# Routing one-hots moved from GpSimd to VectorE, routing steps and a gather moved earlier, in a one-core attention and mixture-of-experts kernel

## The chip, the core and the metric

The kernel runs on one core of a Trainium2 chip. The metric is the device time of one execution in microseconds (us), the median of several executions. Inputs are drawn once and kept.

## What is computed

The reference is block-causal attention over 8 sequences of 576 tokens with 8 heads of width 64, followed by a mixture of 8 experts. A token's expert is its id times a constant, modulo 8, which is the low three bits of the id; no gate is learned, so the routing does not depend on the attention.

```python
scores = scale * np.matmul(q, k.transpose(0, 1, 3, 2))      # 8 x 8 x 576 x 576
scores = np.where(block_i >= block_j, scores, -1000000000.0) # blocks of 64
attn = softmax(scores)
x = (attn @ v) as 4608 x 512
expert_idx = token_ids * np.int64(2654435761) % np.int64(8)
for e in range(8):
    xe = x[expert_idx == e]
    out[expert_idx == e] = np.maximum(xe @ w1[e], 0.0) @ w2[e]   # 512 -> 1024 -> 512
```

## The kernel before, in words

**Attention** is done in 32 pairs of heads, four pairs to a sequence. The loop at L583 runs over steps g = 0 to 33, and g // 4 is the sequence. A step computes the scores of pair g in three chunks (`S_chunk`, L212 and L221, exponential on ScalarE at L238), multiplies the exponentials of pair g - 2 with the values (`PV`, L276 and L279), divides by the row sums (`norm`, L286 and L287) and then makes small pieces of other work in the order in which they are written: transposes of the next sequence's q and k (`T_group`, L180 on TensorE, L187 on VectorE; eight "eighths" per sequence, dealt to the last two or three steps of the sequence before by the table `turned`), the cast of the values on GpSimd (`cast_v`, L155 and L158), loads of sequence b + 2 (`load_seq`, where g is a multiple of 4) and the write of a finished sequence to a DRAM buffer `x_dram` (`write_x`, L301). `fill` (L205) issues products of zeros into a scratch bank; nothing reads them.

**Routing** is a Python generator, `route` (L318). Every `next(rgen)` emits the instructions up to the next `yield`. It extracts the expert of every token, counts tokens per expert with two small matmuls (L353, L354), gives every token a slot (`slot_i`, 640 slots per expert and an overflow area), and then inverts this: for each of the 8 sequences it builds one-hot matrices of the slot's low 7 bits (128 wide) and high part (72 wide, times the two digits of the token's number), and a TensorE product of the two (L465) adds the token numbers into a table in slot order, `tabi`. The one-hots are built on GpSimd by four element-wise instructions each (`equal`, L442 to L447) and a product (L455). Each sequence takes three `next` calls; the loop makes four calls in steps 0 and 1 and one in each later step.

**Experts.** `load_x` gathers the token rows of expert e from `x_dram` into the tile `xg` by indirect DMAs of 128 rows (L310), five per expert. The first three (the early slots, GE = 3) hold only rows of sequences 0 to 5, so they may be gathered before the last two sequences are written; the last two (late) may not. `turn_x` transposes xg (L503, copy at L505), `stage_a` (L655; `stage_a_early` at L510) multiplies by w1 with a ReLU, `stage_b` (L671) by w2, copies the result (L678) and scatters it to the output (L680). During step 29 expert 0's early rows are turned, during steps 30 to 32 its first product is made. After the loop come the late gathers of experts 0 and 1, and then the experts in turn: while expert e is multiplied, w1, w2 and xg of expert e + 2 are requested, in that order. The turns of expert e + 1 stand between the products of expert e's `stage_b`.

**Queues.** Each engine runs its instructions in the order written. GpSimd (POOL) issues the loads of q, k, w1, w2 and all indirect DMAs from the same stream as its arithmetic; SyncE (SP) issues the loads of v and the writes of `x_dram`. A load of k waits until the values of the sequence before it have landed (`after`). Buffers: two of q, k, v, three of each weight and of xg, two score banks, two banks for transposes and one-hot products (`psT`), one output bank pair (`psO`).

## Time and profile before

| | us |
|---|---|
| median of 3 executions | 352.18 (350.62 to 352.39) |
| the profiled execution, its own time | 354.03 |
| its span, first to last instruction | 352.4 |
| TensorE busy (matmul) | 281.5 |
| GpSimd busy | 210.1 |
| VectorE busy | 148.5 |
| ScalarE busy | 144.0 |

The profile gives the busy time of the engines (PE is TensorE, PEld its weight loads, DVE VectorE, ACT ScalarE, POOL GpSimd), the TensorE clock that was granted (PEclk: 1.00 is 2.4 GHz, 0.50 is 1.2 GHz, a mean in between is a mix of the two), and for each idle stretch of an engine which other engine's work ended it. Busy time of a matmul group is modelled, so it is read beside waits, not alone.

### The profile page before, as it was taken

To read this page: it belongs to the slowest core of one execution; us is meant where nothing else is said; L and a number is where in the kernel's file an instruction comes from. 1 tells how busy PE (TensorE), PEld (TensorE's weight loads), DVE (VectorE), ACT (ScalarE), POOL (GpSimd) and SP (SyncE) were. 2 spreads that over 40 slices of the span, in tenths; PEclk is the share of its full clock that TensorE was granted. 3 is DMA by queue.
4 is the path that set the end of the run, shared out by engine and by line. 5 is a ranking of instruction groups with operands and counts; after the bars stand their busy time and mean duration, and the time that the engine had idled before them with its cause. 6 is when DMAs were issued, how large, how long until landed. Compare 5 with 4: busy or idle time off the path is not lost. (4 is left out here: it accounts for less than half of the span.)

```text
span 352.4 us, 7677 instructions
## 1 busy us (share of the span) xinstructions
PE 281.5 (80%) x3218; PEld 181.8 (52%) x3234; DVE 148.5 (42%) x298; ACT 144.0 (41%) x181; POOL 210.1 (60%) x235
## 2 busy tenths in 40 slices
PE   4858888857756865983989891999999999999980
PEld 1526666635535634762665550465656556565630
DVE  3698596647246326762462121313222231405130
ACT  1573868845534723883424330041323314050600
POOL 7224399999999999615202862757475748414140
PEclk9886999998678868797699996799999999999997
DMA  7999998639619716997702799989999999912020
GB/s 111 189 217 187 195 235 162 136 63 199 115 26 202 136 44 159 190 200 173 162 3 84 124 247 237 183 268 178 256 161 274 181 269 174 266 47 114 15 106 30
DMA packets 65111, 55.63 MB, mean 158 GB/s; under 512 B 39973, under 2 KB 53797, under 8 KB 65072
## 3 DMA queue, kind: packets, MB, share of 16 engines
q0 software_dynamic: 22560, 40.90, 55.5%
q1 hardware_dynamic: 42512, 14.20, 18.3%
...
## 5 line engine op out<-in xcount | busy, mean ns | idle before, releaser
L238 ACT ACTIVATE pt<-ps 128x1024 bf16<-128x1024 f32 x96 | 93.4, 1023 | 67.0 <-PE ps L221 65.8
L659 ACT ACTIVATE hT<-hp 128x640 bf16<-128x640 f32 (+2 forms) x70 | 42.9, 613 | 105.7 <-PE hp L655 104.8
L671 PE MATMUL yp<-w2b,hT 128*128 128x512 bf16 x305 | 76.2, 389 | 0.8
L680 POOL DMA_INDIRECT out_dram<-ysb,perm x40 | 39.9, 998 | 52.9 <-DVE ysb L678 24.9
L655 PE MATMUL hp<-xT,w1b 128*128 128x320 bf16 (+2 forms) x472 | 66.7, 296 | 3.8 <-DVE xT L505 3.6
L310 POOL DMA_INDIRECT xg<-x_dram,tabi x40 | 41.0, 1025 | 43.4 <-DMA x_dram<-xs 31.3
L505 DVE COPY xT<-tx 128x512 bf16<-128x512 bf16 x40 | 16.9, 425 | 101.1 <-PE tx L503 101.1
L187 DVE COPY qkT<-tp 128x640 bf16<-128x640 bf16 (+1 forms) x60 | 50.3, 876 | 18.4 <-PE tp L180 18.1
L655 PEld LDWEIGHTS <-w1b 128*128 128x128 bf16 x472 | 45.6, 98 | 22.6 <-issue 5.7
L671 PEld LDWEIGHTS <-hT 128*128 128x128 bf16 x320 | 30.8, 100 | 31.9 <-issue 2.8
L212 PE MATMUL ps<-qkT 64*128 64x512 bf16 (+4 forms) x320 | 43.6, 336 | 3.0 <-ACT pt L238 1.2
L276 PE MATMUL O<-vx,pt 128*128 128x65 bf16 x896 | 44.2, 206 | 2.2 <-DVE xs L287 1.9
L276 PEld LDWEIGHTS <-pt 128*128 128x128 bf16 x896 | 36.2, 105 | 9.3 <-DVE xs L287 3.9
L678 DVE COPY ysb<-yp 128x512 f32<-128x512 f32 x40 | 27.3, 682 | 12.2 <-PE yp L671 12.2
L212 PEld LDWEIGHTS <-qkT 64*128 64x128 bf16 x320 | 19.2, 103 | 18.6 <-issue 6.5
L287 DVE TENSOR_TENSOR xs<-O,rsall 128x640 bf16<-128x640 f32 x32 | 26.4, 824 | 1.1
L221 PE MATMUL ps<-maskq,maskk 64*128 64x64 bf16 x256 | 26.4, 209 | 0.4 <-issue 0.4
L503 PE MATMUL tx<-identbf,xg 128*128 128x128 bf16 x160 | 16.4, 230 | 12.4 <-DMA xg<-x_dram,tabi 12.3
L503 PEld LDWEIGHTS <-xg 128*128 128x128 bf16 x160 | 12.5, 102 | 21.6 <-DMA xg<-x_dram,tabi 13.4
L180 PE MATMUL tp<-identbf,kb 128*64 128x128 bf16 x288 | 16.1, 255 | 4.5 <-DVE qkT L187 3.2
...
L286 DVE RECIPROCAL rsall<-O 128x10 f32<-128x10 f32 x32 | 6.7, 211 | 27.1 <-PE O L279 26.8
...
## 6 DMA issues: line engine op xcount, KB each, us to landing
...
w1b<-in_moe_w_dram POOLq DMA_DIRECT2D x8, 1024.0 KB, 8.3
w2b<-in_moe_w_dram POOLq DMA_DIRECT2D x8, 1024.0 KB, 13.1
...
vf<-in_v_dram SPq DMA_DIRECT2D x16, 64.0 KB, 4.0
xg<-x_dram,tabi POOLq DMA_INDIRECT x40, 10.0
```

The source lines that it names most:

```text
L187: ins = copy(qk[:, :, w, :].rearrange("p h (g j) -> p h g j", j=JR)[:, :, :, j0 + c0 : j0 + c1], tp[:, at[c0] : at[c1 - 1] + 1, :].rearran ...
L212: nc.tensor.matmul(ps[:, m, o0 : o0 + n], lhsT=qk[rows, r, 1, 128 * i : 128 * i + 128], rhs=qk[rows, r, 0, q0 : q0 + n], start=True, stop= ...
L221: nc.tensor.matmul(ps[:, m, o0 : o0 + 64], lhsT=maskk[rows, :], rhs=maskq[rows, :], start=False, stop=True,)
L238: nc.scalar.activation(ptv[:, :, 512 * ch : 512 * ch + 512], ps[:], ACT.Exp, scale=SCALE)
L276: nc.tensor.matmul(dst, lhsT=pt[:, o0 : o0 + 128], rhs=vx[:, h, i, :], start=(i == 0), stop=(i == t))
L310: r = nc.gpsimd.indirect_dma_start(out=xgs[e][:, gg, :], out_offset=None, in_=x_dram[0:rows, :], in_offset=bass.IndirectOffsetOnAxis(ap=ta ...
L503: nc.tensor.transpose(out=tp[:, db, :], in_=xgs[e][:, tt, db * P : (db + 1) * P], identity=identbf[:])
L655: nc.tensor.matmul(hp[:, t, 0:n], lhsT=w1b[:, db, ft * P : (ft + 1) * P], rhs=xT[:, db, p0:p1], start=(db == 0), stop=(db == NKT - 1),)
L659: nc.scalar.activation(hT[:, ft, c0:c1].rearrange("p (t n) -> p t n", n=n), hp[:, 0 : len(parts), 0:n], ACT.Relu)
L671: nc.tensor.matmul(yp[:], lhsT=hT[:, ft, tt * P : (tt + 1) * P], rhs=w2b[:, ft, :], start=(ft == 0), stop=(ft == NFT - 1),)
L678: nc.vector.tensor_copy(ysb[:], yp[:])
L680: ins = nc.gpsimd.indirect_dma_start(out=out[:, :], out_offset=bass.IndirectOffsetOnAxis(ap=perm3[:, gg : gg + 1], axis=0), in_=ysb[:], in ...
```

## The change

The one-hots are built by VectorE, with `is_equal` against a bf16 counting tile `iota_c` in which every number stands five times, so that the five tokens of a partition are the innermost dimension; three VectorE instructions per sequence take the place of nine on GpSimd. They come before the small tables of `route` and take one `next` per sequence. Before the first transposes the generator is now called four times, with 28 zero products among the calls (11 before); the calls left over are dealt to steps by the table STEPS. The arithmetic on `toki` moves behind the first transposes. Sequence 2's transposes are dealt to three steps as those of the later ones are. The early rows of expert 2 are gathered in step 28, its late rows beside those of experts 0 and 1 after the loop. Expert 0's turn moves from step 29 to 28, its first product from steps 30 to 32 to steps 29 to 31.

```diff
@@ -398,6 +398,41 @@
         nc.vector.tensor_copy(slot_i[:].rearrange("p b i -> p (b i)"), slf[:])
         yield
 
+        lo_i = rt.tile([P, 2, T], I32, name="lo_i", tag="i2")
+        nc.vector.tensor_single_scalar(lo_i[:, 0, :], slot_i[:].rearrange("p b i -> p (b i)"), 127, op=ALU.bitwise_and)
+        nc.vector.tensor_single_scalar(lo_i[:, 1, :], slot_i[:].rearrange("p b i -> p (b i)"), 7, op=ALU.arith_shift_right)
+        dig = rt.tile([P, 2, B, 5], BF16, name="dig")
+        nc.vector.tensor_copy(dig[:].rearrange("p z b i -> p z (b i)"), lo_i[:])
...
+        ones_hi = rt.tile([P, NG, 5], BF16, name="ones_hi", tag="oh")
+        hots = rt.tile([P, 2, P + 2 * NG, 5], BF16, name="hots", tag="tid")
+        yield
+        for b in range(B + 1):
+            if b > 0:
+                hot = hots[:, (b - 1) % 2]
+                pt_ = psT.tile([P, 512], F32, name="pt_", tag="tp")
+                for i in range(5):
+                    n = P if i < NT else 64
+                    nc.tensor.matmul(pt_[:, 0 : 2 * NG], lhsT=hot[0:n, 0:P, i],
+                                     rhs=hot[0:n, P:, i], start=(i == 0), stop=(i == 4))
+                if b == 1:
+                    nc.vector.tensor_copy(acc[:], pt_[:, 0 : 2 * NG])
+                else:
+                    nc.vector.tensor_tensor(out=acc[:], in0=pt_[:, 0 : 2 * NG], in1=acc[:], op=ALU.add)
+            if b < B:
+                nc.vector.tensor_tensor(
+                    out=hots[:, b % 2, 0:P, :], in0=dig[:, 0, b, None, :].to_broadcast([P, P, 5]),
+                    in1=iota_c[:], op=ALU.is_equal)
+                nc.vector.tensor_tensor(
+                    out=ones_hi[:], in0=dig[:, 1, b, None, :].to_broadcast([P, NG, 5]),
+                    in1=iota_c[:, 0:NG, :], op=ALU.is_equal)
+                nc.vector.tensor_tensor(
+                    out=hots[:, b % 2, P:, :].rearrange("p (z h) i -> p z h i", z=2),
+                    in0=ones_hi[:, None, :, :].to_broadcast([P, 2, NG, 5]),
+                    in1=tokb[:, b, :, None, :].to_broadcast([P, 2, NG, 5]), op=ALU.mult)
+                yield
+        yield
+
         eo = rt.tile([1, OVT, E], F32, name="eo")
         nc.vector.tensor_tensor(
             out=eo[:], in0=inc[0:1, None, :].to_broadcast([1, OVT, E]),
@@ -425,49 +460,6 @@
         yield
...
-        dif = rt.tile([P, 5, P], BF16, name="dif", tag="oh")
-        hots = rt.tile([P, 2, 5, P + 2 * NG], BF16, name="hots", tag="tid")
-        yield
-
-        def equal(out, z, b, n):
-
-            d = dif[:, :, 0:n]
-            nc.gpsimd.tensor_tensor(
-                out=d, in0=lo_f[:, z, b, :, None].to_broadcast([P, 5, n]),
-                in1=iota_lo[:, None, 0:n].to_broadcast([P, 5, n]), op=ALU.subtract)
-            nc.gpsimd.tensor_tensor(out=d, in0=d, in1=d, op=ALU.mult)
-            nc.gpsimd.tensor_scalar(d, d, -1.0, 1.0, op0=ALU.mult, op1=ALU.add)
-            nc.gpsimd.tensor_single_scalar(out, d, 0.0, op=ALU.max)
-
-        for b in range(B + 1):
-            if b < B:
-                equal(hots[:, b % 2, :, 0:P], 0, b, P)
-            yield
-            if b < B:
-                equal(dif[:, :, 0:NG], 1, b, NG)
-                nc.gpsimd.tensor_tensor(
-                    out=hots[:, b % 2, :, P:].rearrange("p i (z h) -> p i z h", z=2),
-                    in0=dif[:, :, None, 0:NG].to_broadcast([P, 5, 2, NG]),
-                    in1=tokf[:, b, :, :, None].to_broadcast([P, 5, 2, NG]), op=ALU.mult)
-            yield
-            if b > 0:
-                hot = hots[:, (b - 1) % 2]
...
@@ -530,17 +522,12 @@
                    allow_small_or_imprecise_dtypes=True)
-    iota_lo = rt.tile([P, P], F32, name="iota_lo")
-    nc.gpsimd.iota(iota_lo[:], pattern=[[1, P]], base=0, channel_multiplier=0,
+    iota_c = rt.tile([P, P, 5], BF16, name="iota_c")
+    nc.gpsimd.iota(iota_c[:], pattern=[[1, P], [0, 5]], base=0, channel_multiplier=0,
                    allow_small_or_imprecise_dtypes=True)
     toki = rt.tile([P, B, 5], I32, name="toki")
     nc.gpsimd.iota(toki[:], pattern=[[S, B], [P, 5]], base=0, channel_multiplier=1,
                    allow_small_or_imprecise_dtypes=True)
-    tok2 = rt.tile([P, B, 5, 2], I32, name="tok2")
-    nc.vector.tensor_single_scalar(tok2[:, :, :, 0], toki[:], 6, op=ALU.arith_shift_right)
-    nc.vector.tensor_single_scalar(tok2[:, :, :, 1], toki[:], 63, op=ALU.bitwise_and)
-    tokf = rt.tile([P, B, 5, 2], F32, name="tokf")
-    nc.vector.tensor_copy(tokf[:], tok2[:])
     set_fixed()
 
     vparts = {0: load_v(0, firsts[2])}
@@ -560,26 +547,37 @@
     for m in range(2):
         nc.vector.memset(maskk[64 * m : 64 * m + 1, 64:128], NEG)
         nc.vector.memset(maskq[64 * m : 64 * m + 1, :], 1.0)
-    fill(9)
+
+    fill(8)
     rgen = route()
     next(rgen)
-    fill(2)
+    fill(10)
+    next(rgen)
+    fill(10)
+    next(rgen)
+    next(rgen)
     J2 = JR // 2
     T_group(0, 0, J2, 5, psS)
-    fill(1)
     T_group(0, JR, JR + J2, 5, psS)
     fill(1)
     T_group(0, J2, JR, 5, psS)
     fill(1)
     T_group(0, JR + J2, 2 * JR, 5, psS)
     cast_v(0)
+    tok2 = rt.tile([P, B, 2, 5], I32, name="tok2", tag="i2")
+    nc.vector.tensor_single_scalar(tok2[:, :, 0, :], toki[:], 6, op=ALU.arith_shift_right)
+    nc.vector.tensor_single_scalar(tok2[:, :, 1, :], toki[:], 63, op=ALU.bitwise_and)
+    tokb = rt.tile([P, B, 2, 5], BF16, name="tokb")
+    nc.vector.tensor_copy(tokb[:], tok2[:])
 
     turned = {}
     for c in range(1, B):
         f = NP * c
-        for g, ns in (((f - 2, range(0, 4)), (f - 1, range(4, 8))) if c < 3 else
+        for g, ns in (((f - 2, range(0, 4)), (f - 1, range(4, 8))) if c < 2 else
                       ((f - 3, range(0, 2)), (f - 2, range(2, 5)), (f - 1, range(5, 8)))):
             turned[g] = [(c, n) for n in ns]
+
+    STEPS = {0: 4, 1: 3, 4: 1, 8: 1, 9: 1, 12: 1, 13: 1, 16: 1, 20: 1, 21: 1, 22: 1, 23: 1, 24: 1}
     for g in range(NPAIRS + 2):
         b, r = divmod(g, NP)
         turns = list(turned.get(g, ()))
@@ -597,7 +595,7 @@
             S_chunk(g, 1)
         turn(1)
         if g < 2:
-            fill(2)
+            fill(3)
         if g >= 2:
             PV(g - 2, 0)
         if g < NPAIRS:
@@ -614,7 +612,7 @@
         if g >= 2:
             PV(g - 2, 1)
             norm(g - 2)
-        for _ in range(4 if g < 2 else 1):
+        for _ in range(STEPS.get(g, 0)):
             next(rgen, None)
         if r == 1 and g > 1:
             write_x((g - 5) // NP)
@@ -626,15 +624,16 @@
             load_w1(g // 27)
         if g == 24:
             load_w2(0)
-        if g in (NP * EB + 2, NP * EB + 3):
+        if NP * EB + 2 <= g < NP * EB + 5:
             load_x(g - NP * EB - 2, 0, GE)
 
-        if g == 29:
+        if g == 28:
             for tt in range(GE):
                 turn_x(0, tt, psT)
-        if 30 <= g < 33:
-            for ft in ((0, 1, 2), (3, 4, 5), (6, 7))[g - 30]:
+        if 29 <= g < 32:
+            for ft in ((0, 1), (2, 3, 4), (5, 6, 7))[g - 29]:
                 stage_a_early(0, ft)
+    assert next(rgen, None) is None and rgen.gi_frame is None
     att_ctx.close()
 
     ffn_ctx = ExitStack()
@@ -709,7 +708,7 @@
         nc.vector.tensor_scalar(ctl[:, 2:3], nb[:, 0:1], float(-E * G), float(E * G), op0=ALU.mult, op1=ALU.add)
         nc.vector.tensor_single_scalar(ctl[:, 3:4], nov[:], float(E * G), op=ALU.add)
 
-    for e in range(2):
+    for e in range(3):
         load_x(e, GE, G)
     load_w2(1)
     stage_a(1, 0, ES, 2)
@@ -720,7 +719,8 @@
         if e + 2 < E:
             load_w1(e + 2)
             load_w2(e + 2)
-            load_x(e + 2, 0, G)
+            if e > 0:
+                load_x(e + 2, 0, G)
         stage_a(e, ES if e < 2 else 0, CAP)
         if 1 < e + 1 < E:
             new_ffn(e + 1, mx)
```

## Rows read from the trace of the kernel before

**Rows 1.** Busy time by stage: stretch and length, PE, PEld, DVE, ACT, POOL, PEclk, DMA share, GB/s.
```profile
15.70:36.97 21.27, 15.15 (x217) 10.13 (x218) 17.65 (x46) 11.91 (x13) 7.18 (x9) 0.76 1.07 203
36.97:52.00 15.03, 12.39 (x275) 9.37 (x274) 11.81 (x28) 11.82 (x13) 10.69 (x11) 1.00 1.01 200
52.00:140.30 88.30, 61.86 (x1127) 45.31 (x1127) 44.52 (x73) 47.99 (x52) 83.01 (x83) 0.84 0.62 128
140.30:155.20 14.90, 14.50 (x275) 10.69 (x275) 12.47 (x20) 11.97 (x13) 7.75 (x10) 0.81 1.02 176
155.20:185.70 30.50, 22.91 (x324) 15.71 (x325) 12.76 (x26) 12.70 (x16) 7.06 (x7) 0.83 0.57 124
185.70:229.50 43.80, 34.73 (x207) 19.31 (x208) 9.90 (x19) 9.33 (x23) 25.62 (x26) 0.88 0.87 178
229.50:324.40 94.90, 92.47 (x613) 56.39 (x621) 25.52 (x50) 28.16 (x40) 54.32 (x56) 1.00 0.85 200
```

**Rows 2.** The same view by sequence, first and last inside the third stage.
```profile
52.00:66.15 14.15, 13.05 (x283) 9.88 (x284) 10.43 (x18) 11.76 (x13) 13.34 (x15) 1.00 0.70 162
...
115.70:140.30 24.60, 16.45 (x281) 11.97 (x277) 10.97 (x18) 12.13 (x13) 23.10 (x23) 0.78 0.59 121
```

**Rows 3.** Waits of PE from 66 to 141 us: total, times, longest.
```profile
PE pt__1765 L465 <- POOL hots L455: 4.5, 1, 4.5
...
PE pt__2140 L465 <- POOL hots L455: 3.3, 1, 3.3
```

**Rows 4.** VectorE groups, shapes kept apart: busy us, mean ns, idle before.
```profile
L187 DVE COPY qkT<-tp 128x640 bf16<-128x640 bf16 x32 | 28.9, 904 | 12.5 <-PE tp L180 12.2
...
L287 DVE TENSOR_TENSOR xs<-O,rsall 128x640 bf16<-128x640 f32 x32 | 26.4, 824 | 1.1
...
L390 DVE TENSOR_TENSOR cum<-cum,ovm 128x320 f32<-128x320 f32 x1 | 0.5, 491 | 0.0
```

**Rows 5.** Timeline of VectorE and of GpSimd near 141 us: start, duration.
```profile
140.98 2.17 DVE L471 SCALAR_TENSOR_TENSOR tabf<-acc 128x72 f32<-128x72 f32 x1
...
141.15 1.91 POOL L155 CAST vx<-vf 128x2048 bf16<-128x2048 f32 x1
```

**Rows 6.** Timeline of PE at the start.
```profile
1.36 4.02 PE L205 MATMUL fl<-wz 128*128 128x512 bf16 x9 [1.36 <-DVE wz L84]
...
9.72 1.17 PE L180 MATMUL tp<-identbf,kb 128*64 128x128 bf16 x18
...
12.95 0.69 PE L180 MATMUL tp<-identbf,kb 128*64 128x128 bf16 x18
...
15.70 0.39 PE L212 MATMUL ps<-qkT 64*128 64x512 bf16 x2 [1.11 <-DVE et L331]
```

**Rows 7.** Busy time while VectorE works at routing, L331 to L366 and L402 to L410.
```profile
15.49:20.48 4.99, 2.84 (x39) 1.78 (x40) 4.44 (x16) 3.37 (x5) 3.32 (x4) 0.92 1.08 191
...
31.27:32.46 1.19, 0.41 (x8) 0.30 (x7) 1.12 (x7) 1.19 (x2) 0.10 (x1) 1.00 1.14 214
```

**Rows 8.** Timeline of PE at expert 0's first gathered rows.
```profile
165.69 0.61 PE L503 MATMUL tx<-identbf,xg 128*128 128x128 bf16 x4 [4.10 <-DMA xg<-x_dram,tabi]
```

**Rows 9.** Timeline of PE and of POOL around expert 2's gather.
```profile
209.38 1.89 PE L671 MATMUL yp<-w2b,hT 128*128 128x512 bf16 x7
218.58 0.61 PE L503 MATMUL tx<-identbf,xg 128*128 128x128 bf16 x4 [7.31 <-DMA xg<-x_dram,tabi]
218.98 3.62 PE L671 MATMUL yp<-w2b,hT 128*128 128x512 bf16 x8
...
195.71 0.97 POOL L490 DMA_DIRECT2D w2b<-in_moe_w_dram  x1
```

**Rows 10.** DMA issues from 186 to 200 us: KB each, us to landing.
```profile
w2b<-in_moe_w_dram POOLq DMA_DIRECT2D x1, 1024.0 KB, 10.0
```

**Rows 11.** Timeline of POOL and of PE at expert 3's gathered rows.
```profile
232.94 0.98 POOL L680 DMA_INDIRECT out_dram<-ysb,perm  x1 [3.19 <-DMA xg<-x_dram,tabi]
...
240.45 0.39 PE L503 MATMUL tx<-identbf,xg 128*128 128x128 bf16 x4
```

More of the change, by code (lines that the diff above doesn't have):

```diff
@@ L399, in route @@
         yield
+        lo_i = rt.tile([P, 2, T], I32, name="lo_i", tag="i2")
[3 more added lines that the diff above has]
+        nc.vector.tensor_copy(dig[:].rearrange("p z b i -> p z (b i)"), lo_i[:])
+        acc = rt.tile([P, 2 * NG], F32, name="acc", tag="cum")
+        ones_hi = rt.tile([P, NG, 5], BF16, name="ones_hi", tag="oh")
[26 more added lines that the diff above has]
+        yield
         eo = rt.tile([1, OVT, E], F32, name="eo")
@@ L427, in route @@
         yield
-        lo_i = rt.tile([P, 2, T], I32, name="lo_i")
-        nc.vector.tensor_single_scalar(lo_i[:, 0, :], slot_i[:].rearrange("p b i -> p (b i)"), 127, op=ALU.bitwise_and)
-        nc.vector.tensor_single_scalar(lo_i[:, 1, :], slot_i[:].rearrange("p b i -> p (b i)"), 7, op=ALU.arith_shift_right)
-        lo_f = rt.tile([P, 2, B, 5], F32, name="lo_f")
-        nc.vector.tensor_copy(lo_f[:].rearrange("p z b i -> p z (b i)"), lo_i[:])
-        acc = rt.tile([P, 2 * NG], F32, name="acc", tag="cum")
-        dif = rt.tile([P, 5, P], BF16, name="dif", tag="oh")
-        hots = rt.tile([P, 2, 5, P + 2 * NG], BF16, name="hots", tag="tid")
-        yield
-        def equal(out, z, b, n):
-            d = dif[:, :, 0:n]
-            nc.gpsimd.tensor_tensor(
-                out=d, in0=lo_f[:, z, b, :, None].to_broadcast([P, 5, n]),
-                in1=iota_lo[:, None, 0:n].to_broadcast([P, 5, n]), op=ALU.subtract)
-            nc.gpsimd.tensor_tensor(out=d, in0=d, in1=d, op=ALU.mult)
-            nc.gpsimd.tensor_scalar(d, d, -1.0, 1.0, op0=ALU.mult, op1=ALU.add)
-            nc.gpsimd.tensor_single_scalar(out, d, 0.0, op=ALU.max)
-        for b in range(B + 1):
-            if b < B:
-                equal(hots[:, b % 2, :, 0:P], 0, b, P)
-            yield
-            if b < B:
-                equal(dif[:, :, 0:NG], 1, b, NG)
-                nc.gpsimd.tensor_tensor(
-                    out=hots[:, b % 2, :, P:].rearrange("p i (z h) -> p i z h", z=2),
-                    in0=dif[:, :, None, 0:NG].to_broadcast([P, 5, 2, NG]),
-                    in1=tokf[:, b, :, :, None].to_broadcast([P, 5, 2, NG]), op=ALU.mult)
-            yield
-            if b > 0:
-                hot = hots[:, (b - 1) % 2]
-                pt_ = psT.tile([P, 512], F32, name="pt_", tag="tp")
-                for i in range(5):
-                    n = P if i < NT else 64
-                    nc.tensor.matmul(pt_[:, 0 : 2 * NG], lhsT=hot[0:n, i, 0:P],
-                                     rhs=hot[0:n, i, P:], start=(i == 0), stop=(i == 4))
-                if b == 1:
-                    nc.vector.tensor_copy(acc[:], pt_[:, 0 : 2 * NG])
-                else:
-                    nc.vector.tensor_tensor(out=acc[:], in0=pt_[:, 0 : 2 * NG], in1=acc[:], op=ALU.add)
         nc.vector.scalar_tensor_tensor(out=tabf[:], in0=acc[:, 0:NG], scalar=64.0, in1=acc[:, NG:],
```

## The prediction

> **What bounds the kernel now.** The page's busy shares come first, but they are means over stages with different limits (TensorE is the busiest and GpSimd the second, as the table above shows), so I cut the span into stages [rows 1]. The reader should compare the lengths of equal work. Four steps of the attention loop (one sequence) take 15.03 us from 36.97 and 14.90 us from 140.30. The sixteen steps between take 88.30 us, 22.1 us a sequence, and there GpSimd is busy 83.01 us of the 88.30 and the granted clock is 0.84, a mix of 1.2 and 2.4 GHz. By sequence it is plainer: the first takes 14.15 us at clock 1.00, the last 24.60 us with GpSimd busy for 23.10 (the two between are as long as the last) [rows 2]. The waits name the link: from 66 to 141 us TensorE waits six times for GpSimd's one-hots, between 4.5 and 3.3 us each [rows 3]. So in that stage GpSimd's one-hot arithmetic ends last, and TensorE, clocked down in the gaps, is paced by it.
>
> The end of the kernel has another limit. From 229.50 to 324.40 five experts pass in 94.90 us, 18.98 each, with TensorE busy 92.47 [rows 1]: it is the bound there, and the change leaves its work alone. Before that stand two stops for gathered rows: 4.10 us for expert 0 [rows 8] and 7.31 us for expert 2 [rows 9].
>
> **The parts, costed.** The sum is made against the profiled execution's own 354.03 us, 1.85 above the median of 352.18.
>
> *One-hots on VectorE.* All GpSimd one-hot work goes, 72 instructions. GpSimd keeps casts and DMA issues, about 7.75 us of a 14.90 us sequence [rows 1], and paces nothing there. VectorE gets, per sequence, outputs of 640, 360 and 720 elements. No row shows a two-input bf16 instruction of VectorE with both inputs in SBUF. The nearest are 491 ns for 320 elements and 824 ns for 640 in f32 [rows 4], a slope of 1.04 ns an element and 0.16 us fixed. That makes 0.82 + 0.53 + 0.91, some 2.27 us, and with the addition of a 144-element product (0.31 by the same slope) 2.57 us. Runs of five elements cost little: a copy of 640 written in runs of five takes 904 ns [rows 4]. Bounds: half per element would be 1.38 us for the three; wholly on the path, eight times 2.57 are 20.6 us.
>
> I take the full price, as the rows have it, and ask step by step what of it is on the path. A step lasts about 3.6 us (14.3 by four). In steps 4, 8, 12, 16 and 20 VectorE otherwise has only the normalisation, 1.03 us; with 2.57 it is just full, and I put 0.2 us each on the path, 1.0. Steps 9 and 13 also hold copies of 0.9 and 0.7 us: 1.03 + 1.6 + 2.57 = 5.2, an overrun of some 1.8 us each (3.6), because the copies of the following step queue behind the one-hots and TensorE waits for its transpose banks. The small tables (eo to iv) fall in steps 22 and 23, where three copies already fill VectorE: 1.2 us [rows 7] and about as much again, 2.6 on the path. Sum 7.2 us. The products now read weights and columns at a stride of five elements. No row shows a strided read on TensorE: 0.8 us, near the low end because the products are short, with ends 0 and 5 (eight groups of 0.6 us doubled); a stride can't make them shorter. Bare pace: the mean of 15.03, 14.15 and 14.90, 14.7 us a sequence. Sixteen steps then take 58.8 + 7.2 + 0.8 = 66.8 us for 88.3: **-21.5 us**. Ends: 4 x 14.15 = 56.6 (-31.7), and 58.8 + 20.6 + 2.6 + 5 = 87 (-1.3).
>
> DMA sets no other pace: a sequence moves 2.95 MB (q, k, v in, x out), at the 200 GB/s of a full stage [rows 1] 14.7 us, level with the bare pace and under 16.7, so I add nothing.
>
> Against the change: a 72-element VectorE instruction with both inputs in SBUF took 2.17 us, and ended when a GpSimd cast of 1.91 us beside it ended [rows 5]. A one-hot that meets a cast could lose up to 1.9 us; casts come once a sequence and become ready in steps 5, 9 and 13, as the normalisation starts, which hides 1.3 us of it. The Trainium skill (SBUF — State Buffer, "Who interferes with whom") says that a VectorE instruction with two SBUF inputs contends with a GpSimd one that reads SBUF, and the loser blocks for the whole instruction; by that rule the two double-loaded sequences might pay 1.9 us each, an estimate of 4 us on the sum.
>
> *Routing during the first bytes.* Ahead of the first transposes stand 28 zero products (11 before) and the counting. Nine products took 4.02 us, the rate of 1.2 GHz; a group of 18 transposes took 1.17 us at 9.72 and 0.69 at 12.95 [rows 6], so the clock rose in between, after TensorE had worked from 8.8 on. The first transposes queue behind the products in TensorE's order, and so does the counting product, which waits for VectorE. All 28 at the lower level are 12 us from 1.36, and the transposes would start at 13.4, 3.7 late; with the later ones at the higher level they start near 10.2 and run at 0.69, and four VectorE copies of 0.9 us behind each other are the limit. I take the first score product at 15.0 instead of 15.70, **-0.7** (ends -2 and +2.3). The counting itself lies under the load of the first q and k.
>
> In steps 0 to 3 VectorE is busy 17.65 us of 21.27 [rows 1]: it is the path. Out go 5.5 us of counting (4.99 and two additions) and 1.2 of small tables [rows 7]; in come 2.3 for the first one-hots and 0.4 net for moved arithmetic: **-4.0** (ends -2 and -6). Sequence 2's transposes over three steps instead of two: **-0.5**.
>
> *Expert 0 a step earlier.* TensorE stops after step 29 for 4.10 us [rows 8]: the gather waits for sequence 5's write, which shares DMA with weights. Loads of sequence 7 are now done before the weights are asked for, so the write should come through sooner, but the turn asks a step sooner too. I keep 1 us of the stop and count 1.4 us for a clock that stays up (0.83 in this stage [rows 1]): **-4.5** (ends 0 and -8).
>
> *Expert 2 gathered sooner.* Three gathers in step 28 are three more GpSimd issues of 1.3 us, where GpSimd is busy only 7.06 us of 30.50 [rows 1]. Two late gathers more are issued before w2 of expert 1: 2.6 us later for that load. It was issued at 195.71, took 10.0 us and was needed at 209.38 [rows 9, 10], 3.7 us to spare, so nothing is added; without that margin up to 3. The stop of 7.31 us goes, and with it the slow products behind it (3.62 us against 1.89 [rows 9], and 0.8 more): 9.8. Late next is expert 3's gather. Its first rows had landed by 232.94 and were used at 240.45 [rows 11], 7.5 us to spare; TensorE now asks 9.8 us sooner, but 0.39 MB fewer stand ahead, 2.0 us at 200 GB/s. I take 0.8 us of it as paid: **-9.0** (ends -5 and -10).
>
> Sum: 21.5 + 0.7 + 4.0 + 0.5 + 4.5 + 9.0 = 40.2; 354.0 - 40.2 = 313.8, less 1.85 for the median: 312.
>
> **The rivals.** *Cheap one-hots:* 1.38 us for the three. Then of the steps only 9 and 13 overrun, by 0.9 us each; 4.6 us become 1.8, step 1 gains 0.9, and it is 3.7 less, 308. For it: both inputs are 16-bit and contiguous inside. Against it: no row. The Trainium skill (Vector Engine (DVE) Microarchitecture Reference, "Performance modes") says that two-source instructions on 2-byte operands of step one give two results a cycle, also where a row is read again and again; by that rule this rival is the case.
>
> *Wholly on the path:* casts and copies collide with the one-hots everywhere, and 20.6 us count instead of 4.6: 328. Against it: VectorE was busy 10.43 us of 14.15 [rows 2], which leaves room.
>
> *Expert 3's rows late:* the stop moves one expert on and the 9.0 us come back: 321. For it: the DMA share is 0.87 already [rows 1]. Against it: the 7.5 us to spare.
>
> *GpSimd was not the pace:* steps 8 to 23 keep their 88.3 us: 333.5. The waits speak against it [rows 3].
>
> *Slower:* VectorE becomes the bound of the attention loop because a one-hot set costs far more than its elements. All on the path, it must cost over 5.6 us (40.2 + 4.6, by eight) to eat the gain; at 6.5 us the time is 312 + 8 x 6.5 - 4.6 = 359. The copy in runs of five speaks against such a price [rows 4].
>
> **Chances.** Forecast 0.45, cheap one-hots 0.24, wholly on the path 0.12, expert 3 late 0.13, not the pace 0.03, slower 0.03. The range is 302 to 328: its low end is the cheap case with the better ends at the start and in steps 28 to 33, its high end the case wholly on the path. 0.5% (1.8 us) is about what a measurement can tell from no change; every case but the last is faster by far more, and 0.01 is left for the gain and a loss meeting: 0.96, 0.01, 0.03.
>
> **What would show it.** Right: no wait of TensorE for one-hots; attention sequences of 14 to 17 us at a clock near 1.00 with GpSimd below two thirds busy; one-hots of 0.8, 0.5 and 0.9 us (nearly half in the cheap case); no stop of 7 us in expert 1's second product; a first score product near 15 us. Wrong: sequences above 20 us, several us of waits a sequence for VectorE's copies, a start after 17 us, or a new stop at expert 3's turn.

## The result and the profile after

| | before | after |
|---|---|---|
| time, median of four runs (us) | 352.28 (350.62 to 352.78) | 315.74 (313.84 to 317.12) |
| ratio | 1 | 0.8966, 95% interval 0.8909 to 0.9024 |
| profiled execution: its own time, span (us) | 354.03, 352.4 | 317.12, 315.5 |
| mean granted clock | 0.896 | 0.968 |

The forecast was 312 us (302 to 328). The kernels below ran on other chips too, each beside the kernel before, whose median there was 352.5 to 355.2 us; so they are compared by their ratio to it, and 0.01 of ratio is 3.5 us. Three profiles (the zero products cut, the control, both edits) fell on executions some 4 us above the median of their kernels; of these three only times are used.

The stage view of the kernel after, cut at the same work as [rows 1] (steps 0 to 3, 4 to 7, 8 to 23, 24 to 27, 28 to 33, experts 0 and 1, expert 2 to 3, four experts):

```profile
15.04:33.16 18.12, 12.88 (x218) 8.97 (x220) 16.01 (x35) 11.91 (x13) 7.88 (x10) 0.91 1.04 195
33.16:47.60 14.44, 13.07 (x277) 9.72 (x278) 11.55 (x21) 11.75 (x13) 4.07 (x5) 1.00 1.08 197
47.60:113.00 65.40, 55.20 (x1125) 40.76 (x1125) 51.36 (x95) 47.38 (x53) 18.52 (x22) 1.00 1.05 207
113.00:127.24 14.24, 13.54 (x272) 9.83 (x273) 11.77 (x29) 11.86 (x13) 2.64 (x3) 0.88 0.93 194
127.24:155.11 27.87, 21.74 (x324) 14.90 (x325) 12.38 (x26) 12.80 (x16) 10.08 (x10) 0.94 0.42 103
155.11:188.53 33.42, 31.66 (x204) 18.39 (x206) 9.91 (x19) 9.08 (x22) 18.77 (x19) 1.00 0.79 159
188.53:211.43 22.90, 20.36 (x126) 11.78 (x125) 5.20 (x10) 5.62 (x8) 11.88 (x12) 0.93 0.98 223
211.43:287.40 75.97, 74.03 (x492) 45.15 (x498) 20.43 (x40) 22.50 (x32) 46.25 (x48) 1.00 0.91 210
```

Against [rows 1]: the start to the first score -0.7 (15.04 for 15.70), steps 0 to 3 -3.2, 4 to 7 -0.6, 8 to 23 **-22.9**, 24 to 27 -0.7, 28 to 33 -2.6, experts 0 and 1 **-10.4**, expert 2 to 3 **+3.9** (22.90 for 18.98), the rest the same: -37.1 in all. In steps 8 to 23 GpSimd is busy 18.52 us of 65.40 where it had 83.01 of 88.30, VectorE 51.36, the clock is 1.00 and the DMA engines' share 1.05. The waits of TensorE in that stretch hold no one-hots any more ([rows 3]):

```profile
PE tp L180 <- DVE qkT L187: 3.4, 3, 1.2
PE O L276 <- DVE xs L287: 3.1, 5, 1.9
PE ps L246 <- ACT pt L238: 1.8, 4, 0.5
```

The one-hots among VectorE's groups, shapes kept apart (busy, mean ns, idle before):

```profile
L429 DVE TENSOR_TENSOR hots<-ones_hi,tokb 128x720 bf16<-128x720 bf16 x8 | 5.0, 624 | 0.3
L423 DVE TENSOR_TENSOR hots<-dig,iota_c 128x640 bf16<-128x640 bf16 x8 | 4.7, 582 | 0.0
L426 DVE TENSOR_TENSOR ones_hi<-dig,iota_c 128x360 bf16<-128x360 bf16 x8 | 3.3, 413 | 0.0
```

A set costs 0.58 + 0.41 + 0.62 = 1.62 us, not the 2.27 taken. Where no cast of GpSimd runs beside it, it is 0.55 + 0.37 + 0.61 = 1.53. The five matmuls of a product, now read at a stride, take 1.07 us; without the stride (the kernel *tokens outermost* below) they take 0.58, both at full clock:

```profile
51.42 1.08 PE L416 MATMUL pt__1094<-hots 128*128 128x144 bf16 x5
```

```profile
52.44 0.58 PE L416 MATMUL pt__1094<-hots 128*128 128x144 bf16 x5
```

Two new stops appear. In step 10 VectorE's normalisation waits for the write of an earlier sequence's results, which has the same tile. The timelines of VectorE, and of SP's queue some 11 us before:

```profile
63.17 0.83 DVE L287 TENSOR_TENSOR xs<-O,rsall 128x640 bf16<-128x640 f32 x1 [1.93 <-DMA x_dram<-xs]
```

```profile
39.20 9.63 SPq L141 DMA_DIRECT2D vf<-in_v_dram  x4
48.88 2.85 SPq L144 DMA_DIRECT2D vf<-in_v_dram  x2
51.83 1.14 SPq L301 DMA_DIRECT2D x_dram<-xs  x2
```

Six loads of v occupy SP from 39.20 to 51.73, and only then is sequence 0's write issued; it lands 11 us later. The other stop is at expert 3's rows; below it expert 0's, on TensorE's timeline:

```profile
131.84 0.40 PE L495 MATMUL tx<-identbf,xg 128*128 128x128 bf16 x4 [0.82 <-DMA xg<-x_dram,tabi]
133.07 0.40 PE L495 MATMUL tx<-identbf,xg 128*128 128x128 bf16 x4 [0.83 <-DMA xg<-x_dram,tabi]
...
201.72 0.40 PE L495 MATMUL tx<-identbf,xg 128*128 128x128 bf16 x4 [2.06 <-DMA xg<-x_dram,tabi]
201.95 2.67 PE L670 MATMUL yp<-w2b,hT 128*128 128x512 bf16 x8
204.84 2.63 PE L670 MATMUL yp<-w2b,hT 128*128 128x512 bf16 x8
```

Expert 0 stops 1.65 us where it stopped 4.10 [rows 8], expert 2 not at all [rows 9], expert 3 for 2.06, with products of 2.6 us behind it (1.89 at full clock).

### The profile page after: what moved, and what is told of

Same layout as the page of the kernel before. It is cut to its first block, busy times and chain, and to the rows that moved or that the text cites. A ratio compares the mean times of both kernels' runs of the same rounds, so it can differ in the third digit from the quotient of the medians.

```text
span 315.5 us, 7660 instructions
## 1 busy us (share of the span) xinstructions
PE 271.4 (86%) x3235; PEld 175.0 (55%) x3252; DVE 155.3 (49%) x322; ACT 142.9 (45%) x181; POOL 135.1 (43%) x163
## 5 line engine op out<-in xcount | busy, mean ns | idle before, releaser
L670 PE MATMUL yp<-w2b,hT 128*128 128x512 bf16 x305 | 75.2, 385 | 0.8
L497 DVE COPY xT<-tx 128x512 bf16<-128x512 bf16 x40 | 16.8, 424 | 90.3 <-PE tx L495 90.1
L187 DVE COPY qkT<-tp 128x640 bf16<-128x640 bf16 (+1 forms) x60 | 48.9, 871 | 4.0 <-PE tp L180 3.8
L276 PE MATMUL O<-vx,pt 128*128 128x65 bf16 x896 | 40.9, 198 | 5.7 <-DVE xs L287 5.5
L212 PE MATMUL ps<-qkT 64*128 64x512 bf16 (+4 forms) x320 | 38.5, 300 | 6.0 <-DVE qkT L187 2.9
L276 PEld LDWEIGHTS <-pt 128*128 128x128 bf16 x896 | 33.3, 100 | 12.1 <-DVE xs L287 6.8
L677 DVE COPY ysb<-yp 128x512 f32<-128x512 f32 x40 | 27.3, 683 | 13.8 <-PE yp L670 12.2
L155 POOL CAST vx<-vf 128x2048 bf16<-128x2048 f32 x8 | 15.1, 1891 | 37.5 <-PE O L279 34.9
L212 PEld LDWEIGHTS <-qkT 64*128 64x128 bf16 x320 | 18.0, 95 | 18.2 <-issue 4.4
L221 PE MATMUL ps<-maskq,maskk 64*128 64x64 bf16 x256 | 24.3, 191 | 0.0
L112 POOL DMA_DIRECT2D kb<-in_k_dram x9 | 6.7, 749 | 38.6 <-PE tp L180 20.4
L286 DVE RECIPROCAL rsall<-O 128x10 f32<-128x10 f32 x32 | 6.6, 208 | 27.7 <-PE O L279 27.7
L495 PE MATMUL tx<-identbf,xg 128*128 128x128 bf16 x160 | 15.6, 222 | 4.1 <-DMA xg<-x_dram,tabi 3.7
## 6 DMA issues: line engine op xcount, KB each, us to landing
w2b<-in_moe_w_dram POOLq DMA_DIRECT2D x8, 1024.0 KB, 13.6
```

The source lines that it names most:

```text
L187: ins = copy(qk[:, :, w, :].rearrange("p h (g j) -> p h g j", j=JR)[:, :, :, j0 + c0 : j0 + c1], tp[:, at[c0] : at[c1 - 1] + 1, :].rearran ...
L212: nc.tensor.matmul(ps[:, m, o0 : o0 + n], lhsT=qk[rows, r, 1, 128 * i : 128 * i + 128], rhs=qk[rows, r, 0, q0 : q0 + n], start=True, stop= ...
L276: nc.tensor.matmul(dst, lhsT=pt[:, o0 : o0 + 128], rhs=vx[:, h, i, :], start=(i == 0), stop=(i == t))
L495: nc.tensor.transpose(out=tp[:, db, :], in_=xgs[e][:, tt, db * P : (db + 1) * P], identity=identbf[:])
L670: nc.tensor.matmul(yp[:], lhsT=hT[:, ft, tt * P : (tt + 1) * P], rhs=w2b[:, ft, :], start=(ft == 0), stop=(ft == NFT - 1),)
L677: nc.vector.tensor_copy(ysb[:], yp[:])
```

## The experiments

Each is the kernel after with one edit; one more has the last two together. This table cuts the profiled executions at the normalisations on VectorE (the one in step 2 is the first) and at the end of each expert's turned rows, in us:

| kernel | to step 2 | 2 to 4 | 4 to 26 | 26 to 30 | 30 to 33 | experts 0, 1 | expert 2 | four experts | ratio to before |
|---|---|---|---|---|---|---|---|---|---|
| before | 30.3 | 10.1 | 111.4 | 20.0 | 14.1 | 43.8 | 19.0 | 75.9 | 1 |
| after | 28.7 | 7.9 | 87.3 | 16.1 | 15.4 | 33.4 | 22.9 | 75.9 | 0.8966 |
| one-hots on GpSimd | 26.2 | 16.1 | 105.1 | 19.7 | 13.8 | 35.2 | 19.2 | 79.9 | 0.9835 |
| tokens outermost | 28.8 | 7.9 | 91.7 | 19.5 | 13.8 | 34.5 | 19.5 | 80.5 | 0.9196 |
| late routing | 29.7 | 8.6 | 84.2 | 21.3 | 14.1 | 34.5 | 20.0 | 80.7 | 0.9165 |
| old gather | 27.7 | 7.9 | 86.3 | 18.5 | 13.8 | 43.4 | 20.1 | 77.8 | 0.9251 |
| sets doubled | 30.0 | 7.9 | 97.1 | 21.2 | 13.9 | 34.3 | 20.4 | 77.7 | 0.9424 |
| gather first | 28.3 | 7.9 | 86.6 | 21.0 | 14.0 | 34.3 | 21.1 | 77.6 | 0.9059 |
| steps spread | 28.2 | 7.9 | 90.1 | 24.9 | 13.8 | 34.3 | 20.0 | 77.8 | 0.9310 |
| turn later | 28.0 | 7.9 | 87.6 | 16.2 | 13.8 | 33.4 | 21.2 | 76.2 | 0.8885 |
| writes on ScalarE | 27.5 | 7.9 | 100.1 | 16.5 | 13.8 | 34.9 | 19.5 | 75.9 | 0.9258 |

The first four edits ran on one chip, the next three (with the zero products) on another, the last two on a third. On the first two chips the last columns are longer whatever the edit: 77.6 to 80.7 us for four experts instead of 75.9, and 18.5 to 24.9 in steps 26 to 30. So an edit is judged by the columns that it touches; the total holds some 4 to 7 us beside it there. The unchanged kernel after was not run on those two chips, so that the chip makes these columns longer is the likeliest reading and is not shown; why is open. Each kernel has one profile.

**One-hots back on GpSimd**, with their old layout and at other steps; the early routing, the zero products and the early gather are kept.

```diff
-nc.vector.tensor_tensor(out=hots[:, b % 2, 0:P, :], in0=dig[...], in1=iota_c[:], op=ALU.is_equal)
+equal(hots[:, b % 2, :, 0:P], 0, b, P)
...
-    STEPS = {0: 4, 1: 3, 4: 1, 8: 1, 9: 1, 12: 1, 13: 1, 16: 1, 20: 1, 21: 1, 22: 1, 23: 1, 24: 1}
+    STEPS = {0: 4, 1: 3, 3: 1, 6: 1, 9: 1, 12: 1, 15: 1, 18: 1, 21: 1, 23: 1, 24: 3}
```

> One-hots back on GpSimd in their five operations each and with tokens outermost, their eight sets spread over steps 1 to 21; the early routing, the zero products and the early gather are kept. Theory (the set's work on GpSimd sets the pace wherever it stands, but it now starts some 20 us earlier and needs no barrier of steps): eight sets of 9.7 us and 4.6 us of casts and issues for each sequence stretch steps 1 to 24 by 9 to 14 us against the kernel after, 325 to 330 us. Rival (the engine is the whole gain of steps 8 to 23): all 22.9 us of these steps come back, 337 to 340 us. Rival (GpSimd was not the pace): within 2 us of 315.7.

Measured: 348.34 us, ratio 0.9835 (0.9789 to 0.988). Up to step 26 the kernel takes 147.4 us instead of 123.9, 23.5 more: the rival's size, and the theory's 9 to 14 fall. TensorE's waits from 30 to 135 us, and the two dearest of GpSimd's nine groups for one-hots:

```profile
PE pt__680 L426 <- POOL hots L435: 7.5, 1, 7.5
PE pt__2507 L426 <- POOL hots L435: 7.3, 1, 7.3
PE pt__1481 L426 <- POOL hots L435: 3.2, 1, 3.2
```

```profile
L418 POOL TENSOR_SCALAR hots<-dif 128x640 bf16<-128x640 bf16 x8 | 14.5, 1806 | 0.7
L435 POOL TENSOR_TENSOR hots<-dif,tokf 128x720 bf16<-128x720 bf16 x8 | 11.1, 1390 | 0.7
```

The nine groups sum to 9.6 us a set, as I had taken; but six waits make 22.4 us, since each product stands at a fixed step in TensorE's order and stops everything behind it. An earlier start alone buys little in this placing: by step 26 the kernel is 4.4 us ahead of the kernel before (147.4 for 151.8), the kernel after 27.9. GpSimd was the pace.

**Tokens outermost**: still VectorE and bf16, but the digit is spread over the innermost axis with stride 0, and TensorE reads without a stride.

```diff
-hots = rt.tile([P, 2, P + 2 * NG, 5], BF16, name="hots", tag="tid")
+hots = rt.tile([P, 2, 5, P + 2 * NG], BF16, name="hots", tag="tid")
...
-in0=dig[:, 0, b, None, :].to_broadcast([P, P, 5]), in1=iota_c[:]
+in0=dig[:, 0, b, :, None].to_broadcast([P, 5, P]), in1=iota_c[:, None, :].to_broadcast([P, 5, P])
```

> One-hots stay on VectorE in bf16, but with tokens outermost, so that the routing digit is read with stride 0 innermost and TensorE reads the one-hots without a stride. Theory: a set costs 2.3 us instead of 1.6 and a product of five matmuls 0.6 us instead of 1.07, so that 0.7 x 8 = 5.6 us are lost on VectorE, of which under half is on the path, against 0.49 x 8 = 3.9 us won on TensorE: 313.5 to 317.5 us, no difference to speak of. Rival (the layout makes VectorE's price): a set stays at 1.6 us or below and the kernel gains 3 to 4 us, 312. Rival (VectorE is the pace of these steps): a set at 2.3 us or more and 319 to 322.

Measured: 327.18 us, ratio 0.9196 (0.9107 to 0.9284). The groups:

```profile
L429 DVE TENSOR_TENSOR hots<-ones_hi,tokb 128x720 bf16<-128x720 bf16 x8 | 7.3, 908 | 0.3
L423 DVE TENSOR_TENSOR hots<-dig,iota_c 128x640 bf16<-128x640 bf16 x8 | 6.5, 817 | 0.0
L426 DVE TENSOR_TENSOR ones_hi<-dig,iota_c 128x360 bf16<-128x360 bf16 x8 | 4.2, 527 | 0.0
```

0.82, 0.53 and 0.91 us are the prices of the prediction to the digit: bf16 alone makes nothing cheaper, the layout does. A set costs 0.72 us more than an undisturbed one of the kernel after, and each of steps 4, 8, 12, 16 and 20 takes 0.7 us more, though each product is back at 0.58 us. So in those steps the difference is wholly on the path, TensorE's 0.49 us a product was hidden, and the last rival (VectorE is the pace) holds. The sum of 4.4 us over steps 4 to 26 is less plain: the kernel has no wait in step 10 (1.9 us in the kernel after), and two stretches at half clock, from 63 and from 80 us on, where the kernel after has one, from 114.

**Every set computed twice.**

```diff
+                nc.vector.tensor_tensor(out=hots[:, b % 2, 0:P, :], ..., op=ALU.is_equal)
+                nc.vector.tensor_tensor(out=ones_hi[:], ..., op=ALU.is_equal)
+                nc.vector.tensor_tensor(out=hots[:, b % 2, P:, :]..., op=ALU.mult)
```

> Each set of one-hots is computed twice on VectorE into the same tile; the values are the same. It adds 8 x 1.6 = 12.9 us of VectorE's work in steps 1 to 20. Theory (half or less of a set is on the path, as VectorE still has idle time there and TensorE waits only at the transposes' copies and at the norms): 3 to 7 us more, 319 to 323. Rival (every microsecond there is on the path): 12.9 us more, 328 to 329. Rival (wholly hidden): within 1 us.

Measured: 332.63 us, ratio 0.9424 (0.9377 to 0.9472). Steps 4 to 26 take 9.8 us more for seven extra sets of 1.53 (10.7). Here too the sum hides the missing wait of step 10 and stretches at half clock, but step by step it is 1.4 us in steps 4, 8, 12, 16 and 20 and 1.0 in steps 9 and 13: nearly all on the path, so the theory of half falls. Beside the run before, the steps tell how. The time from the normalisation of step 4 to that of step 5 is 4.2 us after, 4.9 with tokens outermost, 5.6 with doubled sets; with the sets on GpSimd it is 3.5. Sets of 1.53, 2.25 and 3.06 us thus cost 0.7, 1.4 and 2.1: the first 0.8 of a set is hidden (beside the addition of a product, 0.3, that comes with it), and all beyond it counts. In steps 9 and 13, which also hold copies of the transposes, it is 5.2 against 3.4 in steps 5 and 17.

**Late routing**: three of the four routing parts go back behind the first scores.

```diff
     fill(8)
     rgen = route()
     next(rgen)
-    fill(10)
-    next(rgen)
-    fill(10)
-    next(rgen)
-    next(rgen)
+    fill(20)
...
-    STEPS = {0: 4, 1: 3, 4: 1,
+    STEPS = {0: 4, 1: 4, 2: 1, 3: 1, 4: 1,
```

> The routing's steps after the first product go back behind the first scores (four in step 0, four in step 1, one in each of steps 2 and 3); the zero products stay as in the kernel after. Theory (routing on VectorE beside the first copies costs PE its waits there): steps 0 to 3 lengthen by 3 to 4 us and the total is 318.5 to 320. Rival (VectorE has room there, and the gain of steps 0 to 3 came from the warmer clock alone): within 1 us of 315.7.

Measured: 324.88 us, ratio 0.9165 (0.9127 to 0.9203). The stage view of this kernel, and that of the kernel after, cut at the normalisations of steps 2, 4 and 26 (and of step 30, for this one):

```profile
0.00:29.68 29.68, 20.38 (x245) 11.78 (x249) 19.40 (x57) 13.30 (x15) 14.91 (x37) 0.94 0.97 172
29.68:38.23 8.55, 6.41 (x142) 4.85 (x141) 7.10 (x14) 5.88 (x7) 1.38 (x3) 1.00 1.10 213
38.23:122.45 84.22, 74.66 (x1550) 55.30 (x1548) 70.46 (x136) 65.06 (x72) 25.28 (x30) 1.00 1.04 207
122.45:143.77 21.32, 15.75 (x243) 10.71 (x240) 8.33 (x17) 11.69 (x13) 10.11 (x10) 0.79 0.61 155
```

```profile
0.00:28.68 28.68, 20.39 (x245) 11.62 (x249) 22.01 (x63) 13.29 (x15) 13.91 (x36) 0.94 0.94 169
28.68:36.60 7.92, 6.53 (x142) 4.96 (x143) 5.13 (x9) 5.88 (x7) 2.63 (x3) 0.99 1.08 204
36.60:123.87 87.27, 76.10 (x1550) 56.00 (x1548) 70.45 (x135) 65.25 (x72) 25.23 (x30) 0.98 1.06 208
```

By step 4 it is 1.6 us late, not 3 to 4; by step 26 it is 1.4 us *ahead*. It has no wait in step 10. Whoever reaches step 10 sooner waits there for sequence 0's write: 1.93 us in the kernel after, 1.61 to 2.66 in four of the edits, and the waits end between 61.4 and 63.2 us in all of these, while kernels that come there at 62.1 us (this one) or later have none. Of the 3.1 us that it makes up between steps 4 and 26, that wait is 1.9; 0.6 stand in step 7, by a cause not shown, and 0.5 in step 23, where the kernel after ran at the lower clock. So most of what the early routing wins is handed back at that wall. The theory falls; the rival's "within 1 us" fits what is seen by step 26, though its reason (a warmer clock) was not tested. The 7 us of the total stand behind step 26, where this edit changes nothing and the clock was 0.79.

**Zero products cut** from 28 to 11.

```diff
-    fill(8)
+    fill(9)
...
-    fill(10)
-    next(rgen)
-    fill(10)
+    fill(2)
     next(rgen)
```

> The zero products between the routing's parts at the start are cut from 28 to 11 in all, as many as the kernel before had there; the routing stays early. Theory (the zero products only fill PE's idle time; what makes the start short is when the first bytes of q and k land): the first scores begin within 0.5 us of 15.04 us, the clock there is lower, and the total is 0 to 1.5 us longer. Rival (they hold the clock up for the first transposes): the first 33 us grow by 2 us or more, 318 us. Rival (they delay the routing's products): 0.5 to 1 us less.

Measured: 319.47 us, ratio 0.9012 (0.8982 to 0.9042), by the ratio 1.6 us above the kernel after's first measurement, and level with the lowest of the others on its chip (319.63). The chips differ by more than the cases do: inconclusive.

**Expert 2's gather back behind its weights.**

```diff
-    for e in range(3):
+    for e in range(2):
         load_x(e, GE, G)
...
-            if e > 0:
-                load_x(e + 2, 0, G)
+            load_x(e + 2, 0, G)
```

> Only the gather of expert 2's rows goes back to its old place, behind the loads of its weights; all else as in the kernel after. Theory (the stops of 7.31 and 3.62 us at expert 2 are what the move removed, less the 3.9 us that expert 3's turn lost): 321 to 324 us, with the two long stops at expert 2 back and none at expert 3. Rival (the stops came from late weights and not from the place of the gather): within 2 us of 315.7. Rival (nothing was lost at expert 3 through the move): 325 to 327.

Measured: 327.46 us, ratio 0.9251 (0.9181 to 0.9322). TensorE at expert 2's rows:

```profile
186.93 0.61 PE L495 MATMUL tx<-identbf,xg 128*128 128x128 bf16 x4 [7.29 <-DMA xg<-x_dram,tabi]
187.33 3.62 PE L670 MATMUL yp<-w2b,hT 128*128 128x512 bf16 x8
```

These are the stop and the product of [rows 9] again (7.31 and 3.62). The column of experts 0 and 1 is 43.4, 8.9 us above its neighbours on that chip (34.5), and expert 2's shows no stop. The move is worth 9 to 10 us gross, and the theory holds for the place of the gain. It does not hold for the 3.9 us lost at expert 3: on this chip the column of expert 2 is 20.1 with the old gather and 19.5 and 20.0 in its neighbours, so here nothing was lost there, as the last rival has it (the total, 327.46, is nearest to it too).

**Gather ahead of the weights** from expert 3 on.

```diff
-            load_w1(e + 2)
-            load_w2(e + 2)
             if e > 0:
                 load_x(e + 2, 0, G)
+            load_w1(e + 2)
+            load_w2(e + 2)
```

> From expert 1 on, the gather of the rows of two experts ahead is issued before the loads of its weights. Theory (expert 3's first products wait 2.06 us for rows that stand behind two weight loads on GpSimd's queue, and the clock drop after it costs the rest): the stage from expert 2 to 3 goes from 22.9 to 19.0 us and the total to 311 to 313. Rival (the rows are late since the memory's bandwidth is full): the stop moves to the weights of expert 3 and the total stays within 1.5 us of 315.7.

Measured: 319.63 us, ratio 0.9059 (0.9018 to 0.9099). Expert 3's rows come in time, but expert 2's column is 21.1 us, longer than its neighbours' 20.0 and 20.4, because of a stop two tiles on. TensorE's line names no cause, but VectorE's does: it could not copy a product out, since its buffer for results still waited for a scatter. TensorE, VectorE and GpSimd:

```profile
209.00 1.89 PE L670 MATMUL yp<-w2b,hT 128*128 128x512 bf16 x8 [1.93 <-issue]
```

```profile
208.26 0.69 DVE L677 COPY ysb<-yp 128x512 f32<-128x512 f32 x1 [2.67 <-DMA out_dram<-ysb,perm]
```

```profile
193.78 0.95 POOL L482 DMA_DIRECT2D w2b<-in_moe_w_dram  x1
195.04 1.06 POOL L679 DMA_INDIRECT out_dram<-ysb,perm  x1 [0.30 <-DMA xg<-x_dram,tabi]
```

There are six such buffers, and the first scatter of expert 1, issued at 195.04 straight behind two weight loads, is the one that frees the buffer; until 208.26 are 13 us. So the stop moved from the rows to the results. The theory's 19.0 us fall. The DMA share is 0.98 in that stretch; that the memory is the limit fits, but is not shown.

**Routing spread** over the steps without copies, small tables to steps 24 and 25.

```diff
-    STEPS = {0: 4, 1: 3, 4: 1, 8: 1, 9: 1, 12: 1, 13: 1, 16: 1, 20: 1, 21: 1, 22: 1, 23: 1, 24: 1}
+    STEPS = {0: 4, 1: 3, 4: 1, 8: 1, 12: 1, 16: 1, 17: 1, 20: 1, 21: 1, 24: 2, 25: 2}
```

> The routing's calls are placed only in steps where no transposed copies are due (4, 8, 12, 16, 20) or one of them is (17, 21), and the small tables move from steps 22 and 23 to 24 and 25. Theory (the one-hots cost the path only where they stand beside the copies of the transposes, and the tables 2.6 us): 2 to 3 us less, 312.5 to 314. Rival (the tables cost the same wherever they stand and the gather of expert 0 now comes late): 315 to 317. Rival (the work is hidden anyway): within 1 us.

Measured: 329.14 us, ratio 0.9310 (0.9281 to 0.9339), slower than every case of the expectation. Steps 9 and 13 do fall from 5.2 to 3.4 us, but step 10 now waits 2.66, steps 17 and 21 take 5.2, and steps 25 and 26 6.5 and 6.2 instead of 3.4 and 3.2. VectorE in step 25, and TensorE behind it:

```profile
120.73 0.72 DVE L448 TENSOR_TENSOR pvalid<-base,jg 128x24 f32<-128x24 f32 x1
...
123.47 0.18 DVE L470 TENSOR_SCALAR perm<-pvalid 128x40 int32<-128x40 f32 x1
123.57 1.47 DVE L187 COPY qkT<-tp 128x640 bf16<-128x640 bf16 x2
```

```profile
124.54 0.74 PE L180 MATMUL tp<-identbf,qb 128*64 128x128 bf16 x10 [2.54 <-DVE qkT L187]
```

A dozen tiny instructions hold VectorE for 2.9 us ahead of a copy that TensorE needs; TensorE stops for 2.54 us, and from 124 to 128 the granted clock is 0.50, in steps 26 to 30 0.63.

**The control and two edits, on a third chip.** The control is the kernel after, unchanged; *turn later* takes expert 0's rows one step later; *writes on ScalarE* takes the results' writes off SP's queue.

```diff
-        if g == 28:
+        if g == 29:
             for tt in range(GE):
                 turn_x(0, tt, psT)
-        if 29 <= g < 32:
-            for ft in ((0, 1), (2, 3, 4), (5, 6, 7))[g - 29]:
+        if 30 <= g < 33:
+            for ft in ((0, 1, 2), (3, 4, 5), (6, 7))[g - 30]:
```

```diff
-            ins = nc.sync.dma_start(dst, src)
+            ins = nc.scalar.dma_start(dst, src)
```

> The kernel after once more, unchanged, beside the three others. In every run so far but the first one of the kernel after, steps 26 to 30 lost about 4 us at half clock behind expert 0's turn, and the experts took 19.5 to 20.5 us each instead of 19.0. Theory (that belongs to the chip or the execution, not to the edits): a ratio of 0.900 to 0.905 to the kernel before, with the low clock behind step 28 in its trace. Rival (it comes from the edits): a ratio of 0.8966 again.

> Expert 0's rows are turned at step 29 and its first product runs in steps 30 to 32, as in the kernel before; all else as in the kernel after. Theory (one step later the rows have landed, so that the stops of 0.8 and 0.8 us go and with them the drop of the clock behind them): 2 to 5 us less than the control. Rival (the clock drops there whatever TensorE waited for): 1 to 1.7 us less. Rival (the work pushed to steps 30 to 33 lands on the path): no gain.

> The attention's results are written to memory through ScalarE's DMA queue instead of SP's, where they stand behind the next sequence's loads of v. Theory (in step 10 VectorE waits 1.9 us for the write of sequence 0, which SP issues 11 us after its data are there): the wait in step 10 goes and the total is 1 to 2 us less than the control. Rival (the issue costs ScalarE as much): within 1 us of the control. Rival (the memory is the limit and the loads of v come late in its place): within 1 us too, with a wait of GpSimd's cast for v.

> Both edits, expert 0's turn one step later and the writes on ScalarE's queue. Theory (they stand in different stages and add up): 3 to 7 us less than the control, a ratio of 0.88 to 0.895 to the kernel before. Rival (what is gained before step 24 is taken back by expert 0's rows or the weights of expert 1): no more than the better one of the two alone.

Measured: control 314.19 us, ratio 0.8906 (0.8882 to 0.8931), so the first measurement holds; that the two edits beside it have short experts too (75.9 and 76.2) fits the reading that the longer ones above belong to the chips. *Turn later*: 313.33, 0.8885 (0.8828 to 0.8943), no difference that the intervals can tell, so the theory's 2 to 5 us fall. The stops for the rows are gone from TensorE's timeline, and what is left is a wait for a copy:

```profile
135.13 0.61 PE L495 MATMUL tx<-identbf,xg 128*128 128x128 bf16 x8
136.79 0.38 PE L495 MATMUL tx<-identbf,xg 128*128 128x128 bf16 x4 [1.05 <-DVE xT L497]
```

But step 26 of it has a new stop for a write of results (VectorE waits 1.89 us for it, TensorE 1.87), and the clock falls to 0.57 behind that one instead.

*Writes on ScalarE*: 326.21, 0.9258 (0.923 to 0.9286), 12.0 us slower than the control, and with both edits 323.74, 0.9169 (0.9135 to 0.9203). The wait in step 10 is gone, as expected, but ScalarE's timeline shows a price far above that of the first rival (an issue as dear as on SP):

```profile
41.62 9.40 ACTq L301 DMA_DIRECT2D x_dram<-xs  x2
51.13 2.91 ACT L238 ACTIVATE pt<-ps 128x1024 bf16<-128x1024 f32 x3 [11.64 <-DMA vf<-in_v_dram]
```

Two issues that took 1.14 us on SP once the loads were through hold ScalarE for 9.40, until the six loads of v that SP was issuing are nearly all out, and the exponentials queue behind them. Step 5 takes 15.0 us instead of 3.4. So it was not the order on SP alone that made the write late: on another engine's queue the issue goes no faster than the loads beside it.

## Why the prediction was right

The total came out 3.7 us above the forecast, inside the range. What ended the waits was forecast rightly: GpSimd's one-hots, and the place of expert 2's gather. That the sizes came so close is in part luck, since the errors inside the terms went both ways.

**One-hots, -21.5; measured -22.9.** The mechanism is shown by the run on GpSimd (23.5 us come back by step 26). Inside the term several sizes were off, and that they cancel to 1.4 us is luck. The *price* of a set was 2.27 and is 1.62, the "cheap one-hots" rival, which had 1.38; its 308 us did not follow. The *0.2 us on the path* in each of steps 4, 8, 12, 16 and 20 is 0.7 at the low price, and would be 1.4 at mine: I filled the whole step of 3.6 us with VectorE's work, but the doubled sets show that only 0.8 us of a set, or 1.1 with the addition, is free. Steps 9 and 13 overrun by 1.8 each, as I had it, at the lower price. The *bare pace* of 14.7 us a sequence was too long: steps without a set or a wait take 3.4, 3.4, 3.2 and 3.6, 13.6 us. With 13.6 x 4 = 54.4, five times 0.7, twice 1.8 and the wait of 1.9 in step 10 it is 63.4, and the tables and the last product make up the rest of the 65.4: 2.0 us, where the tables alone had 2.6. The strided reads, 0.8 in the sum, cost TensorE 0.49 x 8 = 3.9 us, all hidden. And "DMA sets no other pace" does not hold for step 10: at 13.6 us a sequence the transfers, 14.7 by my own estimate, are the longer one, and there a wait of 1.9 us shows. In the rest of steps 8 to 23, at 16.4 us a sequence over the whole stretch, the profile shows no wait of TensorE behind a transfer.

The Trainium skill (Vector Engine (DVE) Microarchitecture Reference, "Performance modes") has two results a cycle for two-byte operands of step one. The two layouts bear out the condition: with the digit at stride 0 innermost the set cost the f32 price, at step one less. Its size was more modest: 0.61 us for 720 elements and 0.37 for 360 make 0.67 ns an element, where half of the 1.04 of [rows 4] would be 0.52. The Trainium skill's rule of contention (SBUF — State Buffer, "Who interferes with whom") had a smaller effect on the one-hots than the 4 us that I worked out from it: the two sets that met casts took 0.68 + 0.55 + 0.67 = 1.90 us instead of 1.53. Such a stop was seen elsewhere: in step 0 a comparison of 320 elements (L387, one input) took 2.02 us and ended 0.2 us after a cast of 1.92 beside it, where it took 0.32 with tokens outermost.

**Start and steps 0 to 3, -4.7; measured -3.8** against the kernel before. But undoing the early routing costs 1.6 us by step 4 and nothing by step 26: what failed is the reading that VectorE's length there is the path to the end. What it wins is mostly waited for at step 10. Which parts make the other 2 us is open. Steps 4 to 7 took 0.6 less, where sequence 2's transposes had 0.5; no run undoes them.

**Expert 0, -4.5; measured -2.6.** I kept 1 us of the stop and it was 1.65; and the 1.4 us for a clock that stays up did not come, since it fell at the end of the stage (0.94). Nor is the gain owed to the earlier step: with the turn one step later, steps 26 to 33 take 30.0 us, the kernel after 31.5, the kernel before 34.1, and the total does not differ. That the write of sequence 5 came through sooner, as I reasoned, fits; no run isolates it.

**Expert 2, -9.0; measured -10.4 + 3.9 = -6.5.** The gross gain is as forecast (9.8), and the run with the old gather has the same stops again. The 0.8 us "taken as paid" for expert 3 was the mis-sized part: its rows stop TensorE for 2.06 us, and the slow clock behind it costs about as much again. So the rival "expert 3's rows late" came true by 40 per cent in this execution, and the new stop at expert 3's turn, named among the signs of being wrong, did come. The size is not a fixed price: with the turn later the same stop is 2.01 us, no low clock follows and the column is 21.2 instead of 22.9; with the tokens outermost, the late routing, the doubled sets, the spread steps and the writes on ScalarE it is 0.4 to 1.2 us and the column 19.5 to 20.4. Against the old gather on its own chip the move wins 9.0 to 9.5 us over experts 0 to 2, which is the forecast. In the kernel after, expert 3's gathers stand on GpSimd's queue behind waits that my 7.5 us to spare left out:

```profile
185.27 1.00 POOL L310 DMA_INDIRECT xg<-x_dram,tabi  x1 [2.04 <-DMA w1b<-in_moe_w_dram]
190.33 1.00 POOL L310 DMA_INDIRECT xg<-x_dram,tabi  x1 [4.06 <-DMA w2b<-in_moe_w_dram]
```
